# S4 convolution with adaLN and a Mish MLP: the rounding constant of the angle products of blocks 1 to 3 as a 65th row

## Chip, cores and metric

One core of one Trainium2 chip runs the whole program in one launch. The metric is device time in microseconds (us); a kernel is run several times and the median is given. Engine names are those of the profile: PE is TensorE's matmul, PEld its weight load, DVE VectorE, ACT ScalarE, POOL GpSimd, SP SyncE. SPq and POOLq are DMA queues that SP and POOL fill.

## What is computed

The reference, cut to what matters (L = 2048 positions, D = 512 channels, N = 128 states, F = 1792):

```python
mod = (silu(c) @ w_mod).reshape(1, 6, 1, -1)          # sa, ca, ga, sb, cb, gb
h = layernorm(x) * (1 + ca) + sa
# S4: K[d,l] = Re sum_n C[d,n] * dt[d]*B[d,n] * exp(dt[d]*A[d,n]*l), l = 0..2047
# y = causal convolution of h with K along the 2048 positions, + h * Dskip
x = x + ga * y
h = layernorm(x) * (1 + cb) + sb
x = x + gb * (mish(h @ w1 + b1) @ w2)
```

## The kernel before, in words

The 512 channels lie in four blocks of 128 (`NB`), each block in eight steps, so that the convolution runs over steps k = 0 to 31 (block k // 8). The exponential is written as a magnitude times cosine and sine of an angle; angles are products of split parameters with split powers. A step goes through these stages:

- `s_ang(k)` (line 538): TensorE writes the angles, in turns, into the PSUM tile `pang`, of which there is one buffer. The fraction of the angle is made by adding and subtracting a large constant, MAGIC: products with `ah`, then a product that adds MAGIC (stored values are rounded there), then the same products with `nah = -ah`, which leave the rounded part with its sign turned.
- `s_sin(k)` (line 567): ACT reads `pang` once for the absolute value and once for the sine, and makes the cosine out of the first, all into `ec`.
- `s_mag`, `s_comb` (lines 574, 583): DVE makes magnitudes (`m<-cf`, from the `cf` that ACT makes of the coarse product `pco`) and multiplies them into `ec` (`ec<-ec,m`, `ec<-ec,co`).
- `s_kgen`, `s_ks`, `s_ka` (lines 594 to 637): TensorE contracts `ec` into the convolution's kernel (`pkg`, `pka`), ACT moves it out.
- The convolution itself: `ug`, `q`, `prod`, `pt`, `pib`, and at the end `z`, through DRAM and back.

Beside the steps run the parameters of the next block. `load_params(b)` (line 347) is one DMA of 128x768 values, 393 KB, into the tile `raw` on SP's queue, and `params(b, stage)` (line 427) is a chain on DVE and ACT on `raw` that ends in `pk`. The stage 0 of block 3 is the six 128x256 products and what follows them, `raw<-raw`. `load_s(b, half)` (line 491) brings `pk` into the layout of the angle products: for block 0 by a product with a selection matrix and a copy by ACT, for the others by small DMAs on POOL (lines 510, 512). The tiles are `S12` (name `s` in the profile) and `S3`. In `S12` for blocks 1 to 3 the two parts e = 0 and e = 1 lie in partitions 0 to 63 and 64 to 127 of one tile.

For blocks 1 to 3 one `s_ang` is, in code order: four products `ah` (two column quarters q, two parts e), four products `rnd` with `oneb` (two constants z, two parts e, 32 rows each), four products `nah`. Part e = 0 uses rows 0 to 63 of the array, part e = 1 rows 64 to 127.

What sets the order: instructions of DVE, ACT and TensorE keep the order in which the program issues them (`InOrder`, line 277). Steps 0 to 5 follow a list written by hand (`at`, `SL`); later ones follow a planner (`_plan`, line 104 on) with due times and waits. SP's and POOL's DMAs are put in their queues by the framework's scheduler, which may move them past each other; on the chip each of these two engines works through its own queue in order. Around 90 to 120 us SP's queue holds the writes `ud<-us` (line 744, the transformed input to DRAM), the load of `raw` for block 3 (line 353), the loads `xp<-in_A_u` (line 382) and the reads `gu<-ud` (line 750). POOL's holds the loads of `S12` and `S3` and, behind them, the two halves of `mi` (line 976, 1 MB each).

From about 160 us to 380 us the convolution's steps 11 to 31 run with TensorE nearly always busy; behind them comes the MLP, which TensorE bounds too and whose products the change leaves as they are.

Of the kernel before, what the change touches and what calls it, by code (L numbers as in the profile page):

```python
# [19 lines left out]
P = 128  # L20
# [8 lines left out]
MAGIC = 12582912.0  # L29
TWO_PI = 6.2831845  # L30
HALF_PI = 1.5707963
NCO = 48
SL = {"p25": 2, "p2": 1, "p3": 3, "ls0": 4, "raw": 2, "p0": 5, "ls1": 8, "co0": 6, "vis": 7}
NUG = 2
MS = [[3, 1], [5, 2], [0, 3]]
# [23 lines left out]
def _plan(k0):  # L59
# [70 lines left out]
        op(("ms", i), "T", n + .5, [("cp", i)], 1)  # L130
        op(("mo", i), "V", n + .9, [("ms", i)], frees=[("ms", i)])

    for i, n, d in ((0, 22.9, ("ms", 2)), (1, 23.9, ("ms", 4)), (2, 25, ("vt", 15)), (3, 30, ("add", 15))):
        op(("lo", i), "S", n, [d, ("lo", i - 1), ("ml", 4)])
    wait = {key: sum((d, n) in ops for d, n, _ in o[3]) for key, o in ops.items()}
    then = {}
# [51 lines left out]
def _constants():  # L188
    r = np.arange(32)
    s = np.arange(64)  # L190
    j = np.arange(64)
    i = np.arange(32)
    th = 2 * np.pi * ((j[None, :, None] * (4 * r[:, None, None] + 1 + 128 * s[None, None, :])) % 8192) / 8192.0
    mf = np.zeros((32, 2, 64, 2, 64))
    mf[:, 0, :, 0, :] = np.cos(th)
    mf[:, 1, :, 0, :] = np.sin(th)
    mf[:, 0, :, 1, :] = -np.sin(th)
    mf[:, 1, :, 1, :] = np.cos(th)
    mf = mf.reshape(32, P, P)
# [36 lines left out]
    return {  # L236
        "su": su.reshape(P, 1024).astype(f),
        "hl": hl.astype(f),
        "mf": np.ascontiguousarray(mf.transpose(1, 0, 2).reshape(P, 32 * P)).astype(f),
        "mi": np.ascontiguousarray(mf.transpose(2, 0, 1).reshape(P, 32, 2, 4, 4, 4).transpose(0, 1, 2, 4, 3, 5)  # L240
                                   .reshape(P, 32 * P)).astype(f),
        "bdk": bdk.reshape(P, 128).astype(f),
        "bdu": np.tile(da, (4, 1)).astype(f),
        "di": np.tile(da.T / 2048.0, (2, 1)).astype(f),
        "dx": dx.reshape(P, 16 * P).astype(f),
        "di4": dj.reshape(P, 256).astype(f),
        "ac": ac.reshape(P, 1024).astype(f),
        "ah": ah.reshape(P, 512).astype(f),
        "mc": np.concatenate([mc.reshape(P, 2, 16, NCO)[..., :32].reshape(P, 2, 512),
                              mc.reshape(P, 2, 16, NCO)[..., 32:].reshape(P, 2, 256)], axis=2).reshape(P, 32 * NCO).astype(f),  # L250
        "sel": np.tile(np.concatenate([np.eye(32, P, 32 * k) for k in range(4)], axis=1), (4, 1)).astype(f),
        "ident": np.eye(P, dtype=f),
        "tap": np.eye(4, 4, dtype=f).repeat(32, axis=1) * (np.arange(P) % 32 == 0).astype(f),
    }
# [18 lines left out]
def s4_block(ctx, tc, io, out):  # L273
# [91 lines left out]
    ac, nac = early[:, 0], early[:, 1]  # L365
    ah, nah = (gen.tile([P, 512], F32R, name=n, bufs=1) for n in ("ah", "nah"))
    mc = [keep.tile([P, 16 * NCO], F32R, tag="ws", name=f"mc{h}", bufs=3) for h in range(2)]
    sel = cv.tile([P, 4, P], F32R, tag="yt", name="sel", bufs=1)
    nc.gpsimd.dma_start(sel, io["sel"].rearrange("p (k m) -> p k m", k=4))
    for h in range(2):  # L370
# [14 lines left out]
    bdk = cst.tile([P, 128], F32, name="bdk")  # L385
    bdu = cst.tile([P, 64], F32, name="bdu")
    di = cst.tile([P, 32], F32, name="di")
    di4 = cst.tile([P, 2, 4, 32], F32, name="di4")
    mf = cst.tile([P, 32, P], F32, name="mf")
    MI = []  # L390

# [99 lines left out]
    def load_s(b, half):  # L491
        pk = PKR[b]
        for g in (half, 2 + half):
            d = slice(32 * g, 32 * g + 32)
            if half == 0 or b == 0:
                for i in (g, g + 1) if b else (g,):
                    S3[b, i] = gen.tile([P, P], F32R, tag="s3", name=f"s3_{b}_{i}", bufs=4)
            S12[b, g] = gen.tile([P, 2, P], F32R, tag="s12", name=f"s12_{b}_{g}", bufs=4)
            if b == 0:
                p = bank("psel")  # L500
                for k in range(4):
                    T.matmul(p[:, :384], sel[d, k, :], pk[d, k:12:4, :], start=(k == 0), stop=(k == 3))
                A.copy(S12[b, g].rearrange("p e n -> p (e n)"), p[:, :256])
                A.copy(S3[b, g], p[:, 256:384])
                continue
            for k in range(4):
                q = slice(32 * k, 32 * k + 32)
                if half == 0:
                    for i in (g, g + 1):
                        nc.gpsimd.dma_start(S3[b, i][q, :], pk[32 * i:32 * i + 32, 8 + k, :])  # L510
                for e in range(2):
                    nc.gpsimd.dma_start(S12[b, g][64 * e + 16 * k:64 * e + 16 * k + 16].rearrange("p h n -> p (h n)"),  # L512
                                        pk[d, k + 4 * e, :])

    CO, PCO = {}, {}
# [22 lines left out]
    def s_ang(k):  # L538
# [3 lines left out]
        if b == 0:  # L542
            o = 8 * (c % 4)
            for e in range(2):
                for w in (ac, nac):
                    for q in range(2):
                        T.matmul(p[:, e, 256 * q:256 * q + 256], S12[b, 2 * q + c // 4][:, e, :],
                                 w[:, 32 * o:32 * o + 256], start=(w is ac and q == 0), stop=(w is nac),
                                 skip_group_check=True)
                    for z in range(2) if w is ac else ():  # L550
# [1 line left out]
                                 start=False, stop=False, skip_group_check=True)  # L552
        h, o = c % 4 // 2, 256 * (c % 2)
        for w in (ah, nah) if b else ():
            for q in range(2):
                for e in range(2):
                    r = slice(64 * e, 64 * e + 64)
                    T.matmul(p[:, e, 256 * q:256 * q + 256], S12[b, 2 * q + c // 4][r, h, :], w[r, o:o + 256],
                             start=(w is ah and q == 0), stop=(w is nah), skip_group_check=True)
            for z in range(2) if w is ah else ():  # L560
                for e in range(2):
                    r = slice(64 * e, 64 * e + 32)
                    T.matmul(p[:, e, :], oneb[r].to_broadcast([32, P]), rnd[r, 2 + z:3 + z].to_broadcast([32, 512]),
                             start=False, stop=False, skip_group_check=True)
        EC[k] = gen.tile([P, 2, 16, 96], F32, tag="ec", name=f"ec{k}", bufs=3)

    def s_sin(k):
# [398 lines left out]
    stats(2)  # L966
    at(0, stats, 0)
    at(0, norm_scales)
    nc.sync.dma_start(di4.rearrange("p h j i -> p (h j i)"), io["di4"])
    at(1, lambda: nc.gpsimd.dma_start(ah, io["ah"]))  # L970
    at(3, lambda: A.mul(nah, ah, -1.0))

    def load_mi():
        MI.append(cst.tile([P, 32, P], F32, tag="mi", name="mi"))
# [14 lines left out]
    for b in range(NB):  # L989
# [10 lines left out]
        if b + 2 < NB:  # L1000
            at(k0 + SL["raw"], load_params, b + 2)
            at(k0 + SL["p0"], params, b + 2, 0)
    late = [lambda: (ln_open(0), s_xp(8 * NB - 4), s_xp(8 * NB - 12)), lambda: [s_xp(8 * NB - 4 + n) for n in (1, 2, 3)],
            lambda: [w1_load(n) for n in range(3)],
            lambda: (ln_load(0, range(NB - 2)), s_xp(8 * NB - 11), s_xp(8 * NB - 10))]
    for n, g in enumerate((4, 5, 6, 7, 0, 1, 2, 3)):
        for h in range(2):
            at(NR[n], norm, 8 * h + g)
# [7 lines left out]
    def mlp_open():  # L1016
        right.close()
        wr = ctx.enter_context(tc.tile_pool(name="wr", bufs=1, side="right"))
        MW["wr"], MW["gbb"] = wr, wr.tile([P, D], F32, name="gbb")
        MW["wt"] = tmp.enter_context(tc.tile_pool(name="wt", bufs=2, side="right"))  # L1020
        for kh in range(2):
            for fh in range(2):
                t = wr.tile([P, 2, 2, FH], F32R, tag=f"w1{kh}{fh}", name=f"w1{kh}{fh}")
# [159 lines left out]
    def drain():  # L1183
# [22 lines left out]
        def inva_half(h, js, rows=P):  # L1206
            for j in js:
                for a in range(4):
                    T.matmul(PIA[b, j][32 * a:32 * a + 32, :], di4[:rows, h, j, :], zt[:rows, h, a, :],
                             start=(h == 0), stop=(h == 1), skip_group_check=True)  # L1210

        def direct():
# [361 lines left out]
```

## Time and profile before

| | |
|---|---|
| runs of the kernel before | 689.50, 691.97, 692.64 us; median 691.97 |
| the profiled execution | 688.38 us, of which its span is 686.6 us |
| granted clock of TensorE, mean | 0.973 |
| TensorE busy (PE) | 627.5 us, 91% |
| DVE busy | 478.5 us, 70% |
| ACT busy | 397.8 us, 58% |
| the chain that ended last | PE 63%, DVE 21%, ACT 7%, DMA 5%, issue 3% |

How to read it: the span is from the first to the last recorded instruction, the execution's own time contains the start and the end around it. The chain that ended last is followed back from the last instruction, each step to what released it; an engine's time counts only where it stands in this chain. A row of a timeline gives the start, the time from first start to last end of the group, engine, line, output<-input, shapes and how many instructions; what stands in brackets is the idle time before it and who ended it. Rows of groups overlap by the modelled ends of pipelined instructions, so differences between starts say what an operation costs, and the lengths a little more than that.

### The profile page before, as it was taken

The page shows a single profiled execution, that of the slowest core. Times are in us where ns is not written, and L with a number is a line of the kernel's source. Part 1 is how long each engine was busy: PE and PEld are TensorE (multiplying, and loading weights), DVE is VectorE, ACT ScalarE, POOL GpSimd, SP SyncE. Part 2 cuts the span into 40 slices and gives each one's busy share as a digit, 9 for nine tenths or more (in the row PEclk, how much of TensorE's full clock was granted, in tenths as well). Part 3 has the DMA queues.
Part 4 walks back from the last instruction along what each step waited for, and adds up shares of the span by engine and source line. Part 5 has one row for each costly group of instructions (what it writes and reads, how often), then busy time and mean ns, then how long its engine had stood idle before and what let it go on. Part 6 is the DMA issues. An engine that isn't in the chain of part 4 may idle for free.

```text
span 686.6 us, 16571 instructions
## 1 busy us (share of the span) xinstructions
PE 627.5 (91%) x6740; PEld 506.0 (74%) x6746; DVE 478.5 (70%) x910; ACT 397.8 (58%) x699; POOL 101.6 (15%) x212
## 2 busy tenths in 40 slices
PE   0559798799989999999999999999999999999997
PEld 0444365577867778777875788889989899898996
DVE  5979947899879996998575899576337723653233
ACT  3477566887797878977652765452435334534231
POOL 2000364045404440000100000010000001000000
PEclk9989887799999999999999999999999999999999
DMA  9946789543348566546897988656324552373232
GB/s 252 202 162 192 180 190 268 154 136 83 80 112 229 134 173 183 166 112 187 224 279 224 311 296 274 229 171 198 114 85 146 182 151 92 93 216 123 93 93 62
DMA packets 108220, 117.55 MB, mean 171 GB/s; under 512 B 12904, under 2 KB 84976, under 8 KB 106992
## 3 DMA queue, kind: packets, MB, share of 16 engines
q1 hardware_dynamic: 93296, 85.62, 43.5%
q0 software_dynamic: 14464, 30.36, 15.5%
q8 instruction: 53, 0.87, 0.6%
q10 hardware_dynamic: 384, 0.52, 0.3%
q14 instruction: 23, 0.19, 0.1%
HBM read 81.85 MB, written 32.51 MB: 167 GB/s over the span
## 4 chain that ended last, share of the span: by engine, by line
PE 63%; DVE 21%; ACT 7%; DMA 5%; issue 3%; SPq 0%; DVEq 0%; ACTq 0%
PE pr L285 25%; PE pp L285 9%; PE pkg L285 6%; PE pang L285 5%; PE pub L285 5%; DVE ec L285 4%; DVE raw L285 4%; PE pib L285 3%; PE pkb L285 3%; ACT ec L285 2%; PE pt L285 2%; PE pia L285 2%; DVE m L285 2%; DMA cT<-in_c 1%; DMA w1s<-in_B_w 1%
## 5 line engine op out<-in xcount | busy, mean ns | idle before, releaser
L285 PE MATMUL pr<-hh,w 128*128 128x256 f32 (+1 forms) x420 | 78.2, 327 | 0.5 <-ACT hh L285 0.5
L285 ACT ACTIVATE ec<-pang 128x1024 f32<-128x1024 f32 x64 | 62.3, 1026 | 27.3 <-PE pang L285 27.2
L285 PEld LDWEIGHTS pr<-hh,w 128*128 128x128 f32 x420 | 66.5, 188 | 12.7 <-ACT hh L285 1.9
L285 DVE TENSOR_TENSOR mh<-x,pr 128x256 f32<-128x256 f32 x63 | 26.4, 419 | 65.2 <-PE pr L285 64.9
L285 PE MATMUL pp<-w,mah 128*128 128x512 f32 x224 | 70.5, 396 | 0.0
L285 PE MATMUL pr<-w,mah 128*128 128x512 f32 x224 | 69.9, 393 | 0.0
L1294 POOL DMA_DIRECT2D w<-w2d x42 | 22.2, 528 | 299.1 <-PE pp L285 201.2
L285 DVE TENSOR_TENSOR ec<-ec,m 128x1024 f32<-128x1024 f32 x64 | 61.2, 957 | 5.6 <-ACT ec L285 3.4
L285 ACT ACTIVATE mh<-mh,b 128x256 f32<-128x256 f32 x63 | 32.1, 510 | 51.3 <-DVE mh L285 51.1
L285 ACT ACTIVATE mh<-pr,b 128x256 f32<-128x256 f32 (+1 forms) x35 | 19.4, 558 | 64.0 <-PE pr L285 64.0
L512 POOL DMA_DIRECT2D s<-pk x96 | 47.6, 502 | 38.5 <-PE pang L285 31.6
L285 DVE TENSOR_TENSOR q<-pkb,ug 128x1024 f32<-128x1024 f32 x32 | 39.1, 1220 | 15.9 <-PE pkb L285 15.7
L285 DVE TENSOR_TENSOR mal<-mh,mah 128x512 fp32r<-128x512 f32 x56 | 38.5, 688 | 14.2 <-ACT mah L285 14.0
L285 DVE TENSOR_TENSOR m<-cf 128x1024 f32<-128x1024 f32 x32 | 39.0, 1218 | 10.9 <-ACT cf L285 10.9
L285 ACT ACTIVATE ug<-pub,gd 128x512 f32<-128x512 f32 x64 | 33.9, 586 | 20.4 <-PE pub L285 20.4
L510 POOL DMA_DIRECT2D s<-pk x48 | 23.9, 502 | 138.6 <-PE pua L285 75.7
L285 PE MATMUL pp<-w,mal 128*128 128x512 f32 x112 | 43.9, 392 | 0.0
L285 PE MATMUL pr<-w,mal 128*128 128x512 f32 x112 | 43.9, 392 | 0.0
L285 PEld LDWEIGHTS pkg<-ec 128*32 128x32 f32 x2048 | 34.8, 115 | 10.7 <-issue 4.5
L285 PEld LDWEIGHTS pp<-w,mah 128*128 128x128 f32 x224 | 38.3, 189 | 4.9
L285 DVE TENSOR_TENSOR x<-x,pr 128x256 f32<-128x256 f32 x42 | 17.6, 419 | 34.7 <-PE pr L285 34.7
L285 PE MATMUL pkg<-ec 128*32 128x64 f32 x2048 | 40.1, 232 | 0.8 <-DVE modp L285 0.5
(170 smaller groups left out, 1419.6 us busy)
## 6 DMA issues: line engine op xcount, KB each, us to landing
w<-w2d POOLq DMA_DIRECT2D x42, 512.0 KB, 3.6
ud<-us SPq DMA_DIRECT2D x64, 128.0 KB, 2.8
gu<-ud SPq DMA_DIRECT2D x32, 256.0 KB, 3.0
zd<-z SPq DMA_DIRECT2D x32, 256.0 KB, 3.6
zt<-zd SPq DMA_DIRECT2D x32, 256.0 KB, 5.1
w2d<-w SPq DMA_DIRECT2D x14, 512.0 KB, 4.0
xf<-x2d SPq DMA_DIRECT2D x16, 256.0 KB, 4.6
x2d<-xp SPq DMA_DIRECT2D x14, 256.0 KB, 3.5
```

Of the source, the lines that this page charges most:

```text
L285: ins = f(*a, **kw)
L510: nc.gpsimd.dma_start(S3[b, i][q, :], pk[32 * i:32 * i + 32, 8 + k, :])
L512: nc.gpsimd.dma_start(S12[b, g][64 * e + 16 * k:64 * e + 16 * k + 16].rearrange("p h n -> p (h n)"), pk[d, k + 4 * e, :])
L1294: nc.gpsimd.dma_start(t, w2d[f])
```

## The change

1. In blocks 1 to 3, MAGIC is no longer a product of its own: `ah` has a 65th row that holds MAGIC (partition 64, one more DMA at the start), and the angle's tiles a 65th row of ones. So the `ah` products have 65 rows. Of the two `rnd` products per part, only the second remains (column 3, which takes MAGIC out again).
2. For that the parts e = 0 and e = 1 can no longer lie below each other in one tile: each has a tile of its own in partitions 0 to 64, in two fixed groups of slots, `sga` and `sgb`, that blocks 0 to 3 share. The row of ones is written once, in `load_s` of block 1, by eight DMAs. All `ah` products use rows 0 to 64, all `nah` products rows 0 to 63, and e is now the outer loop.
3. Block 0's angle products keep their shape; ACT copies their tiles in two halves, four copies more in all.
4. To make room, `di4` is loaded in `mlp_open` in place of the start, and the third part of `w1_load` gets a late entry of its own behind angle 31.

```diff
+    sga = keep.tile([P, NSG, 2, P], F32R, tag="ws", name="sga", bufs=3)
+    sgb = gen.tile([P, 8 - NSG, 2, P], F32R, name="sgb", bufs=1)
+    SG = [[sga[:, i] if i < NSG else sgb[:, i - NSG] for i in (2 * g, 2 * g + 1)] for g in range(4)]
...
-            S12[b, g] = gen.tile([P, 2, P], F32R, tag="s12", name=f"s12_{b}_{g}", bufs=4)
+            S12[b, g] = SG[g]
...
-                A.copy(S12[b, g].rearrange("p e n -> p (e n)"), p[:, :256])
+                for e in range(2):
+                    A.copy(S12[b, g][e][:, 0], p[:, P * e:P * e + P])
...
+            if b == 1:
+                for t in S12[b, g]:
+                    nc.gpsimd.dma_start(t[64:65].rearrange("p h n -> p (h n)"), io["row"][:, :2 * P])
...
         for w in (ah, nah) if b else ():
-            for q in range(2):
-                for e in range(2):
-                    r = slice(64 * e, 64 * e + 64)
-                    T.matmul(p[:, e, 256 * q:256 * q + 256], S12[b, 2 * q + c // 4][r, h, :], w[r, o:o + 256],
+            r = slice(0, 65 if w is ah else 64)
+            for e in range(2):
+                for q in range(2):
+                    T.matmul(p[:, e, 256 * q:256 * q + 256], S12[b, 2 * q + c // 4][e][r, h], w[r, o:o + 256],
                              start=(w is ah and q == 0), stop=(w is nah), skip_group_check=True)
-            for z in range(2) if w is ah else ():
-                for e in range(2):
-                    r = slice(64 * e, 64 * e + 32)
-                    T.matmul(p[:, e, :], oneb[r].to_broadcast([32, P]), rnd[r, 2 + z:3 + z].to_broadcast([32, 512]),
-                             start=False, stop=False, skip_group_check=True)
+            for e in range(2) if w is ah else ():
+                r = slice(64 * e, 64 * e + 32)
+                T.matmul(p[:, e, :], oneb[r].to_broadcast([32, P]), rnd[r, 3:4].to_broadcast([32, 512]),
+                         start=False, stop=False, skip_group_check=True)
...
-    at(1, lambda: nc.gpsimd.dma_start(ah, io["ah"]))
-    at(3, lambda: A.mul(nah, ah, -1.0))
+    at(1, lambda: [nc.gpsimd.dma_start(ah, io["ah"]), nc.gpsimd.dma_start(ah[64:65], io["row"][:, 512:])])
+    at(3, lambda: A.mul(nah[0:64], ah[0:64], -1.0))
```

The order in which TensorE gets the products of one angle of block 1 (the first one, step 8). In these rows `s_1_0` and `s_1_2` are the tiles of the first and the third group of states, one for each column quarter, and "x2" stands for two like rows in sequence. Before:

```order
L285 MATMUL pang<-ah,s_1_0_1079 128x256 x2
L285 MATMUL pang<-ah,s_1_2_1098 128x256 x2
L285 LDWEIGHTS oneb
L285 MATMUL pang<-rnd,oneb 128x512
L285 LDWEIGHTS oneb
L285 MATMUL pang<-rnd,oneb 128x512
L285 LDWEIGHTS oneb
L285 MATMUL pang<-rnd,oneb 128x512
L285 LDWEIGHTS oneb
L285 MATMUL pang<-rnd,oneb 128x512
L285 MATMUL pang<-nah,s_1_0_1079 128x256 x2
L285 MATMUL pang<-nah,s_1_2_1098 128x256 x2
```

And now, where `sga` and `sgb` hold the groups for the first and the second quarter:

```order
L286 MATMUL pang<-ah,sga 128x256
L286 MATMUL pang<-ah,sgb 128x256
L286 MATMUL pang<-ah,sga 128x256
L286 MATMUL pang<-ah,sgb 128x256
L286 LDWEIGHTS oneb
L286 MATMUL pang<-rnd,oneb 128x512
L286 LDWEIGHTS oneb
L286 MATMUL pang<-rnd,oneb 128x512
L286 MATMUL pang<-nah,sga 128x256
L286 MATMUL pang<-nah,sgb 128x256
L286 MATMUL pang<-nah,sga 128x256
L286 MATMUL pang<-nah,sgb 128x256
```

Two `rnd` products with their weight loads are gone; the two neighbours of a pair of `ah` or `nah` products are no longer the two parts on different rows, but two quarters of one part on the same rows.

SP's queue around the load of `raw` for block 3, with the writes of the transformed input ahead of it and the loads and reads behind. Before, from the write ahead of that load:

```order
L744 DMA ud<-us_919 64x4x128 x2
L744 DMA ud<-us_891 64x4x128
L353 DMA raw_1307<-in_par 128x768
L744 DMA ud<-us_1030 64x4x128 x2
L744 DMA ud<-us_1034 64x4x128 x2
...
L744 DMA ud<-us_1210 64x4x128 x2
L744 DMA ud<-us_1214 64x4x128 x2
L744 DMA ud<-us_1218 64x4x128 x2
L744 DMA ud<-us_1222 64x4x128 x2
L382 DMA xp_2481<-in_A_u 32x4x128 x3
L750 DMA gu_1281<-ud 128x4x128
```

And now:

```order
L751 DMA ud<-us_892 64x4x128
L751 DMA ud<-us_920 64x4x128
L751 DMA ud<-us_1031 64x4x128 x2
L751 DMA ud<-us_1035 64x4x128 x2
...
L751 DMA ud<-us_1213 64x4x128 x2
L751 DMA ud<-us_1217 64x4x128 x2
L751 DMA ud<-us_1221 64x4x128 x2
L751 DMA ud<-us_1225 64x4x128 x2
L354 DMA raw_1312<-in_par 128x768
L386 DMA xp_2464<-in_A_u 32x4x128
L757 DMA gu_1284<-ud 128x4x128
```

The load of `raw` for block 3 stood ahead of the last two rounds of `ud` writes; it now stands behind all of them, at the place where the first `xp` load stood. On DVE nothing has changed places: `raw<-raw` of block 3 stands between the same neighbours.

More of the change, by code (lines that the diff above doesn't have):

```diff
@@ L31 @@
 HALF_PI = 1.5707963
-NCO = 48
+NCO, NSG = 48, 3
 SL = {"p25": 2, "p2": 1, "p3": 3, "ls0": 4, "raw": 2, "p0": 5, "ls1": 8, "co0": 6, "vis": 7}
@@ L131, in _plan @@
         op(("mo", i), "V", n + .9, [("ms", i)], frees=[("ms", i)])
-    for i, n, d in ((0, 22.9, ("ms", 2)), (1, 23.9, ("ms", 4)), (2, 25, ("vt", 15)), (3, 30, ("add", 15))):
+    for i, n, d in ((0, 22.9, ("ms", 2)), (1, 23.9, ("ms", 4)), (2, 25, ("vt", 15)), (3, 30, ("add", 15)), (4, 30.5, ("ang", 31))):
         op(("lo", i), "S", n, [d, ("lo", i - 1), ("ml", 4)])
@@ L246, in _constants @@
         "di4": dj.reshape(P, 256).astype(f),
+        "row": np.repeat([1.0, MAGIC], 512)[None].astype(f),
         "ac": ac.reshape(P, 1024).astype(f),
@@ L387, in s4_block @@
     di = cst.tile([P, 32], F32, name="di")
-    di4 = cst.tile([P, 2, 4, 32], F32, name="di4")
+    DI4 = []
     mf = cst.tile([P, 32, P], F32, name="mf")
@@ L511, in load_s @@
                 for e in range(2):
-                    nc.gpsimd.dma_start(S12[b, g][64 * e + 16 * k:64 * e + 16 * k + 16].rearrange("p h n -> p (h n)"),
+                    nc.gpsimd.dma_start(S12[b, g][e][16 * k:16 * k + 16].rearrange("p h n -> p (h n)"),
                                         pk[d, k + 4 * e, :])
@@ L546, in s_ang @@
                     for q in range(2):
-                        T.matmul(p[:, e, 256 * q:256 * q + 256], S12[b, 2 * q + c // 4][:, e, :],
+                        T.matmul(p[:, e, 256 * q:256 * q + 256], S12[b, 2 * q + c // 4][e][:, 0],
                                  w[:, 32 * o:32 * o + 256], start=(w is ac and q == 0), stop=(w is nac),
@@ L968, in s4_block @@
     at(0, norm_scales)
-    nc.sync.dma_start(di4.rearrange("p h j i -> p (h j i)"), io["di4"])
-    at(1, lambda: nc.gpsimd.dma_start(ah, io["ah"]))
-    at(3, lambda: A.mul(nah, ah, -1.0))
+    at(1, lambda: [nc.gpsimd.dma_start(ah, io["ah"]), nc.gpsimd.dma_start(ah[64:65], io["row"][:, 512:])])
+    at(3, lambda: A.mul(nah[0:64], ah[0:64], -1.0))
     def load_mi():
@@ L1003, in s4_block @@
     late = [lambda: (ln_open(0), s_xp(8 * NB - 4), s_xp(8 * NB - 12)), lambda: [s_xp(8 * NB - 4 + n) for n in (1, 2, 3)],
-            lambda: [w1_load(n) for n in range(3)],
-            lambda: (ln_load(0, range(NB - 2)), s_xp(8 * NB - 11), s_xp(8 * NB - 10))]
+            lambda: [w1_load(n) for n in range(2)],
+            lambda: (ln_load(0, range(NB - 2)), s_xp(8 * NB - 11), s_xp(8 * NB - 10)), lambda: w1_load(2)]
     for n, g in enumerate((4, 5, 6, 7, 0, 1, 2, 3)):
@@ L1020, in mlp_open @@
         MW["wt"] = tmp.enter_context(tc.tile_pool(name="wt", bufs=2, side="right"))
+        DI4.append(MW["wt"].tile([P, 2, 4, 32], F32, name="di4", bufs=1))
+        nc.sync.dma_start(DI4[0].rearrange("p h j i -> p (h j i)"), io["di4"])
         for kh in range(2):
@@ L1208, in inva_half @@
                 for a in range(4):
-                    T.matmul(PIA[b, j][32 * a:32 * a + 32, :], di4[:rows, h, j, :], zt[:rows, h, a, :],
+                    T.matmul(PIA[b, j][32 * a:32 * a + 32, :], DI4[0][:rows, h, j, :], zt[:rows, h, a, :],
                              start=(h == 0), stop=(h == 1), skip_group_check=True)
```

## Prediction

> **What bounds the kernel now.** I read the totals first, then the stages, then the chain of waits in the stages that the change touches.
>
> ```profile
> span 686.6 us, 16571 instructions
> PE 627.5 (91%) x6740; PEld 506.0 (74%) x6746; DVE 478.5 (70%) x910; ACT 397.8 (58%) x699; POOL 101.6 (15%) x212
> PE 63%; DVE 21%; ACT 7%; DMA 5%; issue 3%; SPq 0%; DVEq 0%; ACTq 0%
> ```
>
> TensorE is busy 91% of the span, but only 63% of the chain that ended last runs over it, and 21% over DVE. So a saving on TensorE counts in some stages only. The table by stages (columns: busy time of PE, PEld, DVE, ACT, POOL with the number of instructions, then granted clock, DMA share, GB/s) says in which:
>
> ```profile
> 100.00:160.00 60.00, 50.86 (x864) 38.87 (x863) 48.09 (x84) 46.04 (x81) 21.36 (x44) 0.86 0.65 178
> 160.00:220.00 60.00, 57.17 (x971) 45.95 (x972) 52.25 (x76) 49.88 (x87) 17.24 (x36) 0.97 0.46 117
> 220.00:280.00 60.00, 59.55 (x1071) 45.33 (x1070) 51.06 (x58) 48.17 (x85) 17.67 (x36) 1.00 0.66 180
> 280.00:320.00 40.00, 40.00 (x788) 31.82 (x786) 37.90 (x42) 32.31 (x55) 0.00 (x0) 1.00 0.50 137
> ```
>
> TensorE has 9 us without work from 100 to 160, and hardly any from 160 on. The chain agrees. These are some of its rows (start, duration, what):
>
> ```profile
> 123.69 1.23 DVE m L285
> ...
> 159.21 0.70 DVE ug L285
> 160.05 0.63 PE pt L285 x4
> ...
> 165.21 1.09 PE pib L285 x8
> 166.30 1.40 PE pang L285 x12
> ...
> 313.15 1.43 PE pang L285 x12
> ```
>
> From 123.69 the chain runs on DVE up to 159.21, then it passes to TensorE and stays there, but for short stretches of ACT and DVE, until the last angle at 313.15. Between 160 and 320 it lists 17 angles, the first at 166.30 and the last at 313.15. Two things count, then: what delays DVE ahead of 160, and what an angle costs TensorE behind it.
>
> **DVE and the load of block 3's parameters.** The order on SP shows the load of `raw` for block 3 behind all writes `ud`, where the first `xp` load stood. Its place in time before, and that of its new neighbours:
>
> ```profile
> 94.25 0.55 SPq L353 DMA_DIRECT2D raw<-in_par  x1
> ...
> 110.75 4.93 SPq L744 DMA_DIRECT2D ud<-us  x5
> 115.72 3.68 SPq L382 DMA_DIRECT2D xp<-in_A_u  x3
> ```
>
> So it will be issued at about 115.7 in place of 94.25: the last writes wait for data that ACT makes, and nothing behind them passes them. What needs it on DVE, in DVE's fixed order:
>
> ```profile
> 114.08 2.06 DVE L285 TENSOR_TENSOR raw<-raw 128x256 f32<-128x256 f32 x6
> 116.17 0.49 DVE L285 TENSOR_SCALAR raw<-raw 128x128 f32<-128x128 f32 x2
> 116.58 0.75 DVE L285 SCALAR_TENSOR_TENSOR q<-sab,hl,q 128x512 f32<-128x512 bf16 x1
> 117.24 1.94 DVE L285 TENSOR_TENSOR ec<-ec,m 128x1024 f32<-128x1024 f32 x2
> ...
> 119.70 1.22 DVE L285 TENSOR_TENSOR ec<-ec,co 128x1024 f32<-128x1024 f32 x1
> 123.69 1.23 DVE L285 TENSOR_TENSOR m<-cf 128x1024 f32<-128x1024 f32 x1 [2.76 <-ACT cf L285]
> ```
>
> The first use is at 114.08, before the load would even be issued. Behind it on DVE wait stage 0 of block 3, `q`, and the products of `ec`, 6.84 us from 114.08 to 120.92 (119.70 + 1.22), then 2.76 us of idle time, then `m` at 123.69, with which the DVE chain begins. If the load lands at L, `m` starts at L + 6.84 in place of 123.69: nothing is lost up to L = 116.85, and each us beyond costs one.
>
> For L the trace has three groups of issues, each with its time to landing, in turn all loads of `raw`, the `xp` loads from 115 to 120 and the `ud` writes around 109 to 116, and the stretch in which the new load would run:
>
> ```profile
> DMA to landing us min/median/max: 3.4/3.7/5.0
> ...
> DMA to landing us min/median/max: 3.2/5.5/6.1
> ...
> DMA to landing us min/median/max: 2.9/8.4/9.7
> ...
> 112.00:126.00 14.00, 10.18 (x153) 7.44 (x150) 10.58 (x20) 11.93 (x20) 0.00 (x0) 0.50 0.83 276
> ```
>
> The DMA engines are 83% busy there: `mi` (2 MB, issued on POOL from 110.03) and the `ud` writes lie ahead. Earliest: 115.7 + 3.4 (as fast as a `raw` load ever was) = 119.1, a loss of 2.3 us. Latest: 115.7 + 9.7 = 125.4, a loss of 8.6. I take 115.7 + 6.1 (the longest `xp`, nearest in place and time) + 1.4 (393 KB at 276 GB/s; an `xp` has 64 KB) = 123.2, a loss of **6.4 us**. That is an estimate from those rows.
>
> What else shifts: ACT's cast `sab` and the `pub` product behind it wait for `q`, so TensorE has more idle time.
>
> ```profile
> 124.21 0.60 PE L285 MATMUL pub<-su,sab 32*128 32x512 bf16 x1 [3.82 <-ACT sab L285]
> ...
> 126.00:130.00 4.00, 4.00 (x79) 3.30 (x79) 3.76 (x14) 2.88 (x6) 0.00 (x0) 0.80 1.00 271
> ```
>
> The granted clock was 0.50 from 112 to 126 and 0.80 in the 4 us behind. I take the cold stretch to be longer by the same shift and to lie beside DVE's chain: no cost; a few us of half speed that reach behind 160 would cost up to 2 us (rival B). The Trainium skill ("TensorE: Matmul & The Clock Gate", Part 1) says that an idle window of about 3.4 us halves the clock; the 3.82 us of idle time in that row and the 0.50 agree with it, and by it the longer wait only prolongs the cold stretch.
>
> **The angles on TensorE.** One angle before, and block 0's products on all 128 rows, which were never paired:
>
> ```profile
> 99.64 0.50 PE L285 MATMUL pang<-early,s 128*128 128x256 f32 x2
> 100.24 0.82 PE L285 MATMUL pang<-early,s 128*128 128x256 f32 x4
> ...
> 107.57 0.50 PE L285 MATMUL pang<-ah,s 64*128 64x256 f32 x4
> 108.01 0.61 PE L285 MATMUL pang<-rnd,oneb 32*128 32x512 bf16 x4
> 108.55 0.51 PE L285 MATMUL pang<-nah,s 64*128 64x256 f32 x4
> ...
> 600.62 0.88 PE L285 MATMUL pr<-hh,wt 128*128 128x256 f32 x6
> ```
>
> Four `ah` products on two halves of the rows take 0.50 us, no more than two products on all rows: the two halves run at the same time. The order shows that the change puts both parts on rows 0 to 64, so the four now run one after the other, and so do the four `nah`. What one more product of 256 columns costs: from two to four, 0.82 - 0.50 = 0.32, 0.16 each; from two to six in the MLP, 0.88 - 0.50 = 0.38, 0.095 each. I take 0.12. Two more for `ah` and two more for `nah` are +0.48 (0.38 to 0.64). The pair of `rnd` products that goes: all four take 0.54 from start to start (108.01 to 108.55), half of it is 0.27; without the change of rows at either end I take 0.23. Sum per angle: 0.48 - 0.23 = **+0.25 us** (+0.11 to +0.41).
>
> Where the instruction ahead is one on all rows, as `pib` ahead of 166.30, there is something to win back:
>
> ```profile
> 165.14 0.97 PEld L285 LDWEIGHTS pib<-yt,mi 128*128 128x128 f32 x8
> 166.23 0.30 PEld L285 LDWEIGHTS pang<-ah,s 64*128 64x128 f32 x4
> ```
>
> PEld stands still from 166.11 to 166.23, and the angle's first load begins only with the angle. Sixty-five rows use the same arrangement as all rows, so the load may go ahead: at most 0.18 us, what one such load lasts when four of them end after 0.30 with the starts 0.04 apart, so +0.07 there. Of the 17 angles 6 stand behind such a product (`pib`, `pub`, `pmodp`, `pco`). The sum is 11 x 0.25 + 6 x 0.07 = **3.2 us** (with all ends low 11 x 0.11 - 6 x 0.07 = 0.8; all high 17 x 0.41 = 7.0). The other 7 angles of blocks 1 to 3 lie beside DVE's or ACT's chain and cost nothing.
>
> **The rest.** Block 0's tiles are copied in halves:
>
> ```profile
> L285 ACT CAST s<-psel 128x256 fp32r<-128x256 f32 x4 | 1.5, 382 | 6.9 <-PE psel L285 6.9
> L285 ACT CAST s<-psel 128x128 fp32r<-128x128 f32 x4 | 1.1, 285 | 0.0
> ...
> 101.93 7.91 POOL L512 DMA_DIRECT2D s<-pk  x16 [4.73 <-PE pang L285]
> 110.03 1.11 POOL L976 DMA_DIRECT2D mi<-in_mi  x2 [0.19 <-issue]
> ```
>
> Two copies of 0.285 for one of 0.382 are +0.19 by their lengths, less where they overlap; two of the four lie on the start's path: I take +0.1 (0 to 0.4). The eight DMAs of the ones: four find POOL idle; four stand among those at 101.93, of which 16 take 7.91, so they put `mi` back by 4 x 0.49 = 2 us. `mi` is read first by `pib` in the next round, over 20 us later; if it were late, TensorE would wait up to 2 us (counted in B). But it then also runs into the new `raw` load, which speaks for the late end of L. `di4` and the last part of `w1` move to places tens of us ahead of their use and cost nothing; their cover is TensorE's run from 280 to 320, 40.00 us of 40.
>
> **Sum:** 6.4 + 3.2 + 0.1 = 9.7 us. The profiled execution took 688.38 (span 686.6, 1.8 around it), so 698.1; it lies 3.6 below the median of the runs, and on the median 691.97 the sum gives **701.7 us**.
>
> **Rivals.**
>
> A, the other side: the load is in time. Place: DVE at 114.08; price: all of the 6.4 us; it decides at L = 116.85. Then 691.97 + 3.3 = 695.3, not slower by what can be told. For it: the 2.76 us of idle time ahead of `m`, the 94.25 at which the load was issued before, and `mi` 2 us later, which leaves the last `ud` writes a freer queue. Against it: 115.72 + 2.9, the shortest landing of any row above, is 118.6. 12%.
>
> B, more than the forecast: `raw` at the late end, and a TensorE that is still at half clock, or waiting for `mi`, when DVE's chain is through. 691.97 + 8.6 + 3.2 + 2 = 705.8. The 0.50 and 0.80 of the clock speak for it, DVE's unbroken chain to 159 against it. 7%.
>
> C, each of the products waits for its own weights: if on the same rows the next load can't run beside a product, each costs 0.12 + 0.18 = 0.30. Eight of them in place of four pairs: 8 x 0.30 - 4 x 0.12 - 0.23 is 1.7, less 0.2 for loads that are waited for already, 1.5 per angle; 17 x 1.5 = 25, with the stall 724. Against it: the `pr<-hh,wt` row, six products on the same rows with a load each in 0.88, 0.15 apiece. The Trainium skill ("TensorE: Matmul & The Clock Gate", Part 3) states that a weight load overlaps running products only when its row group differs, which is what the change takes away; the row of six speaks against it for products of this size. 3%.
>
> D, the change does what it says and no more: the pairs still run at the same time and only the `rnd` pair goes, 17 x 0.23 = 3.9 less, with the load in time: 688.1. Against it: the rows 0 to 64 of both parts in the order, and DVE's 114.08. 4%.
>
> **How the numbers follow.** My forecast has 74%. Its own range is 2.3 + 0.8 to 8.6 + 7.0 us above the median, 695.1 to 707.6. A lies at its lower edge; D and C stay outside, 7%. The range is 694.5 to 707.5. A measurement of this kernel can tell about 0.5%, 3.5 us, from no change. Faster: D and a little, 5%. Same, 688.5 to 695.4: A and the low corner, 13%. Slower: 82%.
>
> **What would show it.** In the changed profile: the load of `raw` issued near 115.7 and DVE waiting "<-DMA raw<-in_par" for 8 to 10 us ahead of the six products; `m` 6 us later; the chain on TensorE beginning at about 166 in place of 160; an `ah` group of four about 0.24 us longer, the `rnd` group of two in about half the time, an angle of 1.65 in place of 1.40; the six angles ahead of 160 without effect. No wait of DVE for `raw` would prove A; PEld rows inside the angle that follow the products one by one would prove C; `rnd` short and `ah` unchanged, D.

## The result, and the profile after

The changed kernel takes 703.98 us (median of 4 runs, 700.61 to 705.03) against 691.16 us before (median of 4, 689.50 to 692.64). The ratio is 1.0169, with a 95% interval of 1.0142 to 1.0195: 11.7 us slower. The profiled execution took 705.03 us, with a span of 703.1 us. The forecast was 701.7 us, 9.7 us slower, with a range of 694.5 to 707.5.

These are the totals and the shares of the chain, from the page of the changed kernel:

```profile
span 703.1 us, 16501 instructions
PE 636.2 (90%) x6692; PEld 519.7 (74%) x6698; DVE 479.1 (68%) x910; ACT 398.2 (57%) x703; POOL 106.1 (15%) x221
PE 70%; DVE 14%; DMA 6%; ACT 6%; issue 2%; SPq 2%; DVEq 0%; ACTq 0%
```

TensorE executes 48 products fewer (two for each of 24 angles) and is busy 8.7 us longer. The chain has moved from DVE (21% before, 14% now) to TensorE, and a share of SP's queue is new in it.

SP's queue in the changed kernel (start, duration, what):

```profile
89.55 27.26 SPq L751 DMA_DIRECT2D ud<-us  x31
116.91 1.65 SPq L354 DMA_DIRECT2D raw<-in_par  x1
118.60 0.88 SPq L386 DMA_DIRECT2D xp<-in_A_u  x1
```

DVE around the same time; in brackets the idle time ahead of a group and what ended it:

```profile
115.76 1.22 DVE L286 TENSOR_TENSOR m<-cf 128x1024 f32<-128x1024 f32 x1
125.55 2.08 DVE L286 TENSOR_TENSOR raw<-raw 128x256 f32<-128x256 f32 x6 [8.57 <-DMA raw<-in_par]
...
128.06 0.75 DVE L286 SCALAR_TENSOR_TENSOR q<-sab,hl,q 128x512 f32<-128x512 bf16 x1
...
132.32 1.22 DVE L286 TENSOR_TENSOR m<-cf 128x1024 f32<-128x1024 f32 x1
```

The load of block 3's `raw` is issued at 116.91 and DVE waits 8.57 us for it. In place of the 2.76 us of idle time ahead of the second `m` there is none now, and that `m` starts at 132.32 in place of 123.69.

One angle of the changed kernel on TensorE, the first that stands behind `pkg` in the chain from 160 on (before, the same stretch is three groups of 4):

```profile
185.64 0.39 PE L286 MATMUL pang<-ah,sga 65*128 65x256 f32 x1
185.86 0.52 PE L286 MATMUL pang<-ah,sgb 65*128 65x256 f32 x3
186.31 0.39 PE L286 MATMUL pang<-rnd,oneb 32*128 32x512 bf16 x2
186.63 0.38 PE L286 MATMUL pang<-nah,sga 64*128 64x256 f32 x1
186.85 0.51 PE L286 MATMUL pang<-nah,sgb 64*128 64x256 f32 x3
```

The second `ah` starts 0.22 us behind the first, where two of one pair used to start 4 ns apart. In the chain most angles now have one of two lengths:

```profile
146.93 1.09 PE pt L286 x4
...
176.20 1.46 PE pang L286 x10
...
185.71 1.65 PE pang L286 x10
...
318.42 1.67 PE pang L286 x10
```

1.65 us stands against 1.40 before; behind a product on all rows (`pib` ahead of 176.20) it is 1.46. The chain passes from DVE to TensorE at 146.93 and not at 160.05: from there on TensorE is the late one, with a lower granted clock than before. This is the stage from 134 to 150, of the changed kernel and then of the kernel before (PE, PEld, DVE, ACT, POOL, then clock, DMA share, GB/s):

```profile
134.00:150.00 16.00, 12.59 (x196) 10.54 (x184) 15.42 (x32) 11.10 (x20) 0.00 (x0) 0.82 0.10 29
```

```profile
134.00:150.00 16.00, 14.51 (x275) 12.03 (x274) 15.58 (x21) 13.80 (x23) 3.21 (x7) 1.00 0.28 78
```

The profiled executions are 16.65 us apart (705.03 and 688.38), 5 us more than the medians' ratio gives. Where those 5 us are from is the last experiment below.

### The profile page after: what moved, and what is told of

The parts are those of the page before. It is cut to its first block, busy times and chain, and to the rows that moved or that the text cites. A ratio compares the mean times of both kernels' runs of the same rounds, so it can differ in the third digit from the quotient of the medians.

```text
span 703.1 us, 16501 instructions
## 1 busy us (share of the span) xinstructions
PE 636.2 (90%) x6692; PEld 519.7 (74%) x6698; DVE 479.1 (68%) x910; ACT 398.2 (57%) x703; POOL 106.1 (15%) x221
## 4 chain that ended last, share of the span: by engine, by line
PE 70%; DVE 14%; DMA 6%; ACT 6%; issue 2%; SPq 2%; DVEq 0%; ACTq 0%
PE pr L286 31%; PE pp L286 10%; PE pkg L286 6%; PE pang L286 5%; PE pub L286 5%; DVE raw L286 4%; PE pkb L286 3%; PE pib L286 3%; DVE ec L286 3%; PE pt L286 2%; ACT ec L286 2%; DVE m L286 1%; PE pia L286 1%; DMA cT<-in_c 1%; DMA raw<-in_par 1%
## 5 line engine op out<-in xcount | busy, mean ns | idle before, releaser
L286 PEld LDWEIGHTS pr<-hh,wt 128*128 128x128 f32 x252 | 35.6, 190 | 5.0 <-DVE mh L286 1.6
L286 DVE TENSOR_TENSOR ec<-ec,co 128x1024 f32<-128x1024 f32 x32 | 39.0, 1218 | 0.0
```

The source lines that it names most:

```text
L286: ins = f(*a, **kw)
```

## The experiments

The theory is that of the prediction: the larger part is DVE's wait for the load that was moved, the smaller part the loss of the pairs on TensorE. The rivals: the wait only hides another delay (the eight DMAs of the ones, the later `mi`); the loss on TensorE comes from the 65th row, from the separate tiles or from the order of the products and not from the rows they share.

### The changed kernel with the load early

```diff
-        "lp": load_params,
+        "lp": lambda b: None,
...
+    at(4, load_params, 3)
```

> The changed kernel with one thing moved: the load of block 3's raw is called earlier in the program, so that SP's queue has it ahead of the last two rounds of ud writes, as before the change. The order of all other engines is the changed kernel's. Theory (the late load is the larger part of the loss): DVE no longer waits for the load, m starts near 125 us and not at 132.3, the chain passes to TensorE near 160 again, and the time falls by about 7.5 us, to some 4 to 5 us above the kernel before (695 to 696, ratio 1.006); the angles stay at 1.65 us. Rival (DVE's wait only takes the place of a delay that the eight DMAs of the ones, the later mi or the colder TensorE make anyhow): another wait ends at the same time and the time stays above 700 us.

Measured: 695.06 us against 691.77, ratio 1.0052 (1.0029 to 1.0074). DVE:

```profile
115.28 2.06 DVE L286 TENSOR_TENSOR raw<-raw 128x256 f32<-128x256 f32 x6
...
125.31 1.22 DVE L286 TENSOR_TENSOR m<-cf 128x1024 f32<-128x1024 f32 x1 [3.18 <-ACT cf L286]
```

No wait for `raw` is left, `m` starts at 125.31, and the idle time ahead of it is back. The place of one DMA in SP's queue is worth 1.0169 - 1.0052 = 1.17%, some 8 us of 11.7 (5.7 to 10.5 with both intervals). The rival is out: no other delay of that size stood behind the wait.

### The kernel before with the load late

```diff
-        nc.sync.dma_start(t[:, 0:6, :], io["par"][b].rearrange("p (k n) -> p k n", k=6))
+        ld = nc.sync.dma_start(t[:, 0:6, :], io["par"][b].rearrange("p (k n) -> p k n", k=6))
+        if b == 3:
+            after(ld, US["last"].ins)
```

> The kernel before with the load of block 3's raw put behind the last ud write on SP by a dependency of order; in its old place the scheduler puts the first load of w1s, the other engines keep their order. Theory: the load is issued near 116 and lands near 124, DVE waits 8 to 9 us for it, and the time is 7 us above the kernel before (698, ratio 1.010), with angles of 1.40 us. Rival (without the change's other parts the queue is free and the load lands by 117): within 2 us of the kernel before.

Measured: 696.78 us, ratio 1.0072 (1.0046 to 1.0097), 5 us slower, less than expected.

```profile
122.86 2.08 DVE L285 TENSOR_TENSOR raw<-raw 128x256 f32<-128x256 f32 x6 [8.89 <-DMA raw<-in_par]
...
129.64 1.22 DVE L285 TENSOR_TENSOR m<-cf 128x1024 f32<-128x1024 f32 x1
```

The load is issued at 115.34 here and DVE goes on at 122.86, 2.7 us ahead of the changed kernel's 125.55. Most of these 2.7 us are older than the load: at 106, where none of this has begun, the same products (found by their place in the order) of the changed kernel's profile run 2.0 us behind those of the first profile of before, and those of this profile 0.0. Without that, `m` is late by 6.0 us here and by 6.6 in the changed kernel. So the one move alone makes the kernel slower, with no other part of the change. Its price is 5 us here (3.2 to 6.7) and some 8 above (5.7 to 10.5); the two intervals overlap, and no run shows a cause for the rest.

### What the load waits for

POOL takes one element of `raw` into each half of `mi`, so that `mi` is loaded only when `raw` has landed:

```diff
         MI.append(cst.tile([P, 32, P], F32, tag="mi", name="mi"))
+        for h in range(2):
+            nc.gpsimd.tensor_copy(MI[0][0:1, 16 * h, 0:1], raw[3][0:1, 0, 0:1])
```

> The changed kernel with one thing added: ahead of the two loads of mi POOL copies one element of block 3's raw into each half of mi (it is overwritten by the load), so that mi starts only when raw has landed. All queues keep their order. Theory (raw lands late not only because it is issued late but because the 2 MB of mi, issued 4 us ahead of it, share the DMA engines with it): raw lands 4 to 5 us after its issue near 117 and not 8.6, DVE's m starts near 128 and not at 132.3, and the time is 4 us below the changed kernel (ratio 1.011). Rival (what it waits for are the ud writes ahead of it in its own queue): landing and time as in the changed kernel, ratio 1.017.

Measured: 699.30 us against 691.68, ratio 1.0109 (1.0072 to 1.0147).

```profile
114.56 0.56 SPq L354 DMA_DIRECT2D raw<-in_par  x1
```

```profile
119.50 2.08 DVE L286 TENSOR_TENSOR raw<-raw 128x256 f32<-128x256 f32 x6 [4.70 <-DMA raw<-in_par]
...
126.28 1.22 DVE L286 TENSOR_TENSOR m<-cf 128x1024 f32<-128x1024 f32 x1
```

The load is issued 2.3 us earlier, but 2.0 of these are not `mi`'s: at 106, ahead of any load of `mi`, this profile is as far ahead of the changed kernel's already. What `mi` does shows at the other end: DVE goes on 4.9 us after the issue in place of 8.6. By the ratios (1.0169 - 1.0109 = 0.6%) some 4 us are gone, so the 2 MB of `mi` on another queue made up about half of the 8 us that the late load costs. What is left goes with its late issue. The Trainium skill ("DMA: Bandwidth & Descriptors", Queues, rings and completion order) says that each DMA engine takes turns between the queues that have work for it, a packet at a time; a load that slows down another queue's transfers agrees with it.

### Is it the order of the products?

The two inner loops of the kernel before, exchanged:

```diff
-            for q in range(2):
-                for e in range(2):
+            for e in range(2):
+                for q in range(2):
```

> The kernel before with the two inner loops of the angle products exchanged (e outer, q inner), all products the same, on the same halves of the rows: of four neighbours the first two now lie on rows 0 to 63 and the last two on rows 64 to 127. Theory (products run at the same time only where neighbours lie on different rows): only the middle two still overlap, three turns in place of two for ah and for nah, 0.24 us more per angle (1.64), 11 x 0.24 + 6 x 0.24 = up to 4 us more in all (ratio 1.004 to 1.006). Rival (the array finds the partner by itself across the neighbours, and the changed kernel's loss comes from its 65 rows): angles of 1.40 and no difference, ratio 1.000.

Measured: 693.71 us against 691.77, ratio 1.0015 (0.9997 to 1.0034): no difference. My expectation was wrong.

```profile
177.28 0.51 PE L285 MATMUL pang<-ah,s 64*128 64x256 f32 x4
177.72 0.61 PE L285 MATMUL pang<-rnd,oneb 32*128 32x512 bf16 x4
178.26 0.51 PE L285 MATMUL pang<-nah,s 64*128 64x256 f32 x4
```

Four products still take 0.44 us from start to start. The starts of single products show two pairs (0, 0.006, 0.223 and 0.229 us), though the code gives first both of one half and then both of the other. These rows don't name the halves; those of a_e1_high below have the same order of loops and do: what counts is that there is work for the other half of the rows close behind, not that it is the next product.

### Is it the rows, the tiles or the 65th row?

Two kernels with the changed kernel's slots and separate tiles and with the fold undone (64 rows, two `rnd` pairs). In the first both parts stay on rows 0 to 63:

```diff
-            r = slice(0, 65 if w is ah else 64)
+            r = slice(0, 64)
...
-                T.matmul(p[:, e, :], oneb[r].to_broadcast([32, P]), rnd[r, 3:4].to_broadcast([32, 512]),
+                    T.matmul(p[:, e, :], oneb[r].to_broadcast([32, P]), rnd[r, 2 + z:3 + z].to_broadcast([32, 512]),
```

> The changed kernel with the fold undone and the new layout kept: ah products of 64 rows, and the rnd pair that adds the constant back in its place. On SP some loads beyond 300 us change places. Theory (a rnd pair costs 0.23 us, a 65th row nothing): angles of 1.88 us in place of 1.65, and 0.4 more behind products on all rows since the 64 rows can't have their weights loaded ahead; 11 x 0.23 + 6 x 0.41 = 5 us above the changed kernel (709, ratio 1.024). Rival (the pair costs nothing, since its loads and products hide behind the change of rows): the changed kernel's time, ratio 1.017.

In the second part e = 1 goes back to partitions 64 to 127, and the row of ones is gone:

```diff
-            r = slice(0, 65 if w is ah else 64)
+                r = slice(64 * e, 64 * e + 64)
...
-                    nc.gpsimd.dma_start(S12[b, g][e][16 * k:16 * k + 16].rearrange("p h n -> p (h n)"),
+                    nc.gpsimd.dma_start(S12[b, g][e][64 * e + 16 * k:64 * e + 16 * k + 16].rearrange("p h n -> p (h n)"),
```

> The changed kernel with the fold undone and part e = 1 moved back to partitions 64 to 127, but in its own slots: separate tiles, e outer, 64 rows, two rnd pairs, no row of ones. raw is still loaded behind all ud writes. Theory (the angles' loss comes from both parts lying on the same rows, not from separate tiles, slots or order): angles of 1.40 to 1.41 us in pairs, and a time 2.5 to 3 us below the changed kernel (700 to 701, ratio 1.013). Rival (slots and separate tiles cost): angles over 1.6 us, ratio 1.017 or more.

Measured: 708.68 us, ratio 1.0233 (1.0207 to 1.0258) for the first; 697.84 us against 691.68, ratio 1.0087 (1.0054 to 1.0120) for the second. An angle in the chain of the first, and of the second:

```profile
177.37 1.87 PE pang L286 x12
```

```profile
184.53 1.41 PE pang L286 x12
```

Same tiles, same number and shape of products, and 0.46 us between them: the rows decide, and neither the tiles nor the 65th row. The first lies 0.64%, 4.4 us, above the changed kernel (5 expected). A `rnd` pair costs 1.88 (most angles of the first) - 1.65 = 0.23 us and the fold does save that. It saves 0.23 and gives up 0.47. The second fell by more than expected, 5.7 us below the changed kernel and not 2.5 to 3. DVE's wait for `raw` is also 1 us shorter there (7.59 us in place of 8.57); the eight DMAs of the ones are gone from it too, but no run takes them out alone. The remaining 1 to 2 us lie within the two intervals.

The second run's tiles also show the order of the starts. This is its first angle of block 1, whose four `ah` products stand in the code as in the changed kernel, `sga`, `sgb`, `sga`, `sgb` (part e = 0, then part e = 1):

```profile
109.33 0.39 PE L286 MATMUL pang<-ah,sga 64*128 64x256 f32 x2
109.56 0.28 PE L286 MATMUL pang<-ah,sgb 64*128 64x256 f32 x2
```

Both `sga` products, the first and the third in the code, start ahead of the second: each starts with its partner on the other half of the rows.

### Pauses at a change of rows, and a kernel that beats both

Inside an angle of the kernel before the starts are not even: behind the `rnd` products comes a step of 0.31 us where 0.22 is the rule. `rnd` uses 32 rows, its neighbours 64. In the kernel before, `rnd` on 64 rows:

```diff
-        nc.gpsimd.memset(rnd[:, z:z + 1], (1 - 2 * (z % 2)) * MAGIC / (P, 32)[z // 2])
+        nc.gpsimd.memset(rnd[:, z:z + 1], (1 - 2 * (z % 2)) * MAGIC / (P, 64)[z // 2])
...
-                    r = slice(64 * e, 64 * e + 32)
-                    T.matmul(p[:, e, :], oneb[r].to_broadcast([32, P]), rnd[r, 2 + z:3 + z].to_broadcast([32, 512]),
+                    r = slice(64 * e, 64 * e + 64)
+                    T.matmul(p[:, e, :], oneb[r].to_broadcast([64, P]), rnd[r, 2 + z:3 + z].to_broadcast([64, 512]),
```

> The kernel before with the rnd products on 64 rows each in place of 32 (the constant per row is halved, the sum is the same), so that ah, rnd and nah all use the same halves of the rows. Starts inside an angle of the kernel before are 0, 0.22, 0.435, 0.66, 0.97, 1.19 and 1.405 us: the steps at each change of rows are longer than they need be, 0.31 in place of 0.22 behind the last rnd. Theory (a change of the row pattern costs some 0.1 us, twice per angle): angles of 1.2 to 1.3 us, 2 to 3 us less in all (689, ratio 0.996). Rival (the pause belongs to the change of data type or to the first product of another kind): angles of 1.40, ratio 1.000.

Measured: 687.03 us against 691.68, ratio 0.9924 (0.9898 to 0.9951), 5 us faster than the kernel before.

```profile
176.74 0.50 PE L285 MATMUL pang<-ah,s 64*128 64x256 f32 x4
177.09 0.61 PE L285 MATMUL pang<-rnd,oneb 64*128 64x512 bf16 x4
177.34 0.59 PE L285 MATMUL pang<-nah,s 64*128 64x256 f32 x4
```

```profile
167.44 1.12 PE pang L285 x12
176.81 1.12 PE pang L285 x12
```

An angle takes 1.12 us in place of 1.40, more than expected: 0.09 less ahead of `rnd` (177.09 - 176.74 = 0.35, before 0.44) and 0.2 less behind it. 17 x 0.28 = 4.8 us agrees with the measured 691.68 - 687.03 = 4.65. The data types are unchanged, so that rival is out. The Trainium skill ("TensorEngine Tiling (Array Packing)", Key Properties) says that a change of the tiling mode drains TensorE, without a price; here two such changes cost 0.28 us.

The same question on the changed kernel, with the early load: everything on all rows, nothing in pairs.

```diff
-            r = slice(0, 65 if w is ah else 64)
+            r = slice(0, 65)
...
-                r = slice(64 * e, 64 * e + 32)
-                T.matmul(p[:, e, :], oneb[r].to_broadcast([32, P]), rnd[r, 3:4].to_broadcast([32, 512]),
+                T.matmul(p[:, e, :], oneb.to_broadcast([P, P]), rnd[:, 1:2].to_broadcast([P, 512]),
...
-    at(3, lambda: A.mul(nah[0:64], ah[0:64], -1.0))
+    at(3, lambda: [A.mul(nah[0:64], ah[0:64], -1.0), A.mul(nah[64:65], ah[64:65], 0.0)])
```

> The changed kernel with the early load of raw, and every product of an angle on the whole array: rnd on all 128 rows (constant split over 128), nah on 65 rows with a zero in the last. So nothing runs in pairs, and no product is on another pattern of rows than its neighbour. Theory (a change of the row pattern costs 0.1 us or more): an angle is 8 x 0.12 + 2 x 0.22 = 1.40 us in place of 1.65, and the time is 17 x 0.2 to 0.25 = 3.5 to 4 us below the one with the early load alone (691, ratio 0.999 to 1.000). Rival (what b_rnd64 gained was only rnd products that ran beside nah): 1.65 to 1.9 us per angle, ratio 1.005 to 1.010.

Measured: 693.14 us against 691.63, ratio 1.0031 (1.0017 to 1.0046).

```profile
170.81 1.40 PE pang L286 x10
180.18 1.58 PE pang L286 x10
```

Behind a product on all rows (`pib` ahead of 170.81) the angle takes the 1.40 us expected; behind products on other rows 1.58 to 1.60, where a change of rows ahead of it stays. That was left out of the expectation, and so the gain over the early load alone is 0.2% and not 0.5%, with intervals that overlap a little. Without pauses inside it, then, an unpaired angle is as long as one of the kernel before, and the paired form without pauses, 1.12 us, is shorter than both.

### The 5 us between the profiled executions

Both kernels profiled once more, unchanged.

> The kernel before, unchanged, for a second profile. In the changed kernel's profile the MLP's products shift by 3.5 us more between 430 and 446 us, against the first profile of the kernel before. Theory (that step is variation from run to run): this profile differs from the first one there by 1 us or more. Rival (the change causes it by its later loads of w1): this profile agrees with the first within 0.3 us.

> The changed kernel, unchanged, for a second profile. Theory (variation): the step of 3.5 us between 430 and 446 us is at most half as large. Rival: 3 to 4 us again.

Measured: 691.56 us and 703.04 us, 11.5 us apart, as the medians are. Lateness of the same product, found by its place in the order:

| place (time in the first profile of before) | second profile of before against the first | changed kernel, second against second of before |
|---|---|---|
| `pkg` at 106.0 | +1.2 | +0.5 |
| `pt` at 138.3 | +1.3 | +7.0 |
| `pt` at 144.3 | +1.3 | +9.5 |
| `pt` at 160.05 | +1.3 | +8.9 |
| `pib` at 165.9 | +1.3 | +8.9 |
| `pib` at 325.2 | +1.3 | +11.8 |
| `pr` at 393.0 | +1.3 | +11.2 |
| `pr` at 446.2 | +2.5 | +11.3 |
| `pr` at 674.4 | +3.2 | +11.3 |

The first profile of the kernel before is a favourable one: the kernel before differs from itself by 1.3 us before 130 and by 1.9 more behind 430, and the changed kernel's second profile has a step of 1.2 there in place of 3.5. The theory holds; the later loads of `w1` cost nothing that these show. About half of the early 1.3 us comes in block 0's first angle. It took this long in the first profile of before, and in the second:

```profile
28.59 0.63 PE L285 MATMUL pang<-rnd,oneb 128*128 128x512 bf16 x2
28.88 0.83 PE L285 MATMUL pang<-early,s 128*128 128x256 f32 x4
```

```profile
28.86 1.08 PE L285 MATMUL pang<-rnd,oneb 128*128 128x512 bf16 x2
29.37 1.25 PE L285 MATMUL pang<-early,s 128*128 128x256 f32 x4
```

The same instructions with the same data took up to 1.7 times as long (1.08 us against 0.63, 1.25 against 0.83). That would fit a lower clock, but the granted clock of the profile is 1.00 in both there, so the cause is not shown.

## Why the prediction was right, step by step

The sign, the range and both mechanisms held, and a third term that the sum put at nothing cost 1.9 us; it is most of what lies between the 9.7 us forecast and the 11.3 to 11.7 measured. By the second pair of profiles the 11.3 us divide into 0.5 ahead of 106, 6.5 up to `pt` at 138.3 (`raw`), 1.9 (TensorE from there to 166), 2.9 (angles from 166 to 326) and -0.5 behind.

- **The load's place and DVE's wait.** Forecast: issued at 115.7, landed at 123.2, `m` 6.4 us late. Measured: issued at 116.9, DVE goes on at 125.26 to 125.55, `m` 7.0 us late in the second pair (132.03 against 124.99), 6.5 without the 0.5 that were there at 106. So the loss came out as forecast, but with some luck in its terms. The second profile of the changed kernel runs 1.7 us behind the first of before at 106; without these, the load is issued at 115.2 and DVE goes on at 123.5. From issue to use are 8.4 us and not the 7.5 of the sum, and an issue 0.5 us earlier than forecast makes up for half of that. `mi` was put back by 2.0 us in the second pair (111.3 to 113.3), as forecast.
- **The longer cold stretch of TensorE.** Forecast: it lies beside DVE's chain and costs nothing. This step failed: `pt` at 160.05 is 8.9 us late where `m` is 7.0 late, so 1.9 us are lost (1.2 in the first pair). Not the cold stretch that was there before costs them, but a second one behind it. This is the changed kernel by stages, the second of them the new cold stretch:

```profile
134.00:144.00 10.00, 7.18 (x122) 5.84 (x113) 9.48 (x26) 8.30 (x16) 0.00 (x0) 1.00 0.15 45
144.00:151.40 7.40, 6.81 (x86) 5.92 (x87) 7.33 (x8) 2.80 (x5) 0.00 (x0) 0.54 0.01 2
151.40:162.00 10.60, 10.60 (x187) 8.75 (x186) 10.22 (x16) 8.06 (x15) 5.00 (x10) 1.00 0.69 190
```

The clock is back at 1.00 from 134. Then TensorE waits 2.82 us for `ec`, which DVE makes late because of `raw`, and the clock falls again. Its products in the changed kernel, and the same ones in the kernel before:

```profile
143.93 1.89 PE L286 MATMUL pkg<-ec 128*32 128x64 f32 x64 [2.82 <-DVE ec L286]
...
146.93 1.09 PE L286 MATMUL pt<-ident,ug 128*128 128x128 f32 x4 [0.59 <-DVE ug L286]
147.81 1.91 PE L286 MATMUL pkb<-mf,gk 128*128 128x128 f32 x8
```

```profile
138.30 0.63 PE L285 MATMUL pt<-ident,ug 128*128 128x128 f32 x4 [1.49 <-DVE ug L285]
138.76 1.06 PE L285 MATMUL pkb<-mf,gk 128*128 128x128 f32 x8
```

TensorE is idle right ahead of `pt`, so no work had piled up: the lateness grows from 7.0 to 9.5 while these products take nearly twice as long, and falls to 8.9 at 160, where TensorE of the kernel before had still waited for DVE. With the early load (a_raw_early) the clock is 1.00 from 138 to 146; with the late load in the kernel before (b_raw_late) TensorE waits 2.88 us and the clock is 0.50 from 142 to 148. So the second cold stretch belongs to the late load, and is part of its 8 us. Rival B came near this with a TensorE at half clock and "up to 2 us", but had it behind a `raw` at the late end. The 3.82 us of idle time to which the prediction put the 0.50 do not begin it, for the clock is 0.50 from 112 on and that idle time lies behind 120.
- **The angles.** Forecast +0.25 each and +0.07 behind a product on all rows, 3.2 us in all. Measured +0.25 (1.65 against 1.40) and +0.06 (1.46), and 2.9 us from 166 to 326. The bounds of 0.8 to 7.0 were wider than they needed to be.
- **Rival C** (each product waits for its own weights, 724 us): the changed kernel's products on the same rows follow each other at 0.12 us, after one step of 0.20 to 0.22, each with a load of its own (the first at 185.64, three more in 0.43 us from 185.75), so the loads do run beside products there. The rule of the Trainium skill ("TensorE: Matmul & The Clock Gate", Part 3), overlap only with another row group, doesn't hold for these.
- **The rest.** The copies of block 0 can't be told from the 1.3 us by which the start varies. The four DMAs of the ones among the loads of block 1 may have cost something, by way of `mi` and `raw`; no run shows it by itself.

Not tried: the changed kernel's products with `rnd` on 64 rows in pairs. What begins the stretches of half clock stays open as well: one stands behind 2.82 us of idle time, none behind 1.49 in the kernel before, and in a_mi_wait a shorter one behind two waits of 0.43 and 1.53 us.

## What to carry to other kernels

A fold that removes a product is paid for if it breaks what let the rest run in pairs: count turns on the array, not products. Look at what an edit does to queues that it doesn't mean to touch: of 11.7 us, some 8 came from one load that a scheduler put behind 24 others, and calling the load earlier brings them back. And let neighbouring products use the same rows: giving the small product twice the rows it needs made the kernel 0.76% faster, and folding half of it away left it 0.5% slower even with the load in its old place.

## What was not expected of the hardware

- Two changes of the row pattern inside an angle (64, 32, 64 rows) cost 0.28 us of 1.40.
- Products on different halves of the rows run at the same time even if the code gives both of one half first (starts at 0, 0.006, 0.223 and 0.229 us).
- A 393 KB load whose landing took 3.4 to 5.0 us elsewhere took 7.5 (b_raw_late) to 8.6 us (the changed kernel) behind and beside 2 MB on another queue, and under 5 without them.
- A wait of TensorE of 2.82 us was followed by some 7 us of half clock, which cost 1.9 us on a stage where another engine had been the late one.
